# Letting attention run on into the z1 stage, loading spatial weights as their region frees, and two smaller reorderings, in a fused attention and spatial-gating kernel

## The chip, the cores and the metric

One NeuronCore of a Trainium2 chip runs the whole program. The metric is the device time of one execution in microseconds (us), lower is better.

## The reference, cut to what matters

```python
def reference(A_x, A_wqkv, A_wo, B_x, B_w_in, B_w_sp, B_b_sp, B_w_out, gate_w):
    # x: 1 x 2048 x 1024, all bf16
    g = sigmoid((A_x * gate_w).sum(-1, keepdims=True))
    # A: 32 heads of 32, each position attends to 8 positions at distance 0, 2, ... 14
    a = softmax(mask(q . k_gathered * scale)) . v_gathered, then @ wo
    # B: z = gelu(x @ w_in); z1 = first half (1792 columns), z2 = layernorm(second half)
    gsp = w_sp @ z2 + b_sp            # w_sp: 2048 x 2048
    b = (z1 * gsp) @ w_out
    return g * a + (1 - g) * b
```

The kernel runs, in this order: gate and q/k/v products with the scores of attention, z2, z1, the spatial product with w_sp, and the output. TensorE works nearly without a break; attention's weighted sums run beside it on VectorE (DVE), from about 45 to about 300 us.

## The kernel before

All large products are one-level Strassen products: seven smaller products, each of four 128x128 weight loads, whose results are shared and added in PSUM by ScalarE (ACT) and DVE. Every product asks for a bank from `bank_roles`, and ACT copies ("seeds") and evicts between them. A small planner with clocks for each engine interleaves deferred work (`fill`, `due`, `streams`).

**Banks and score blocks.** In group 2 the score blocks stand behind products 1, 3 and 5 of a q/k quad; then the v quads begin:

```python
            if n + 1 in (BAND_AT if g != 2 else (1, 3, 5)):   # BAND_AT = (1, 3, 6)
                band_set(g, x)
# ...
        if g == 2:
            first = v_quad(0)
            for _ in range(2):
                next(first)
                step()
            mark(bank_roles[1][1:3], VH)     # two short matmuls, L558
            run(v_quad(1), first, step=step)
```

**Gate rows.** Two stores of gate rows are issued ahead of everything that follows the first scores:

```python
    sync.dma_start(... g_d ..., g_s[:])
    gate_dma = sync.dma_start(... og_d ..., omg_h[:])
    settle()
    # ... first gathers of scores are planned after this
```

**The z1 stage.** Seven steps (`fp` 0 to 6) of 12.08 us. Attention is forced to end (`drain`) after the second, and the first eight blocks of the spatial weights are loaded with DMA transposes at fixed places of the third, fourth and fifth:

```python
    DRAIN, SUMS = 1, NFH - 2
    RAW_AT = {2: {2: 0, 4: 1}, 3: {2: 2, 4: 3, 6: 4}, 4: {2: 5, 4: 6, 6: 7}}
    for fp in range(NFH):
        # ...
        hooks = {3: lambda: mark(late, 512, ZC),
                 **{n: lambda a=a: load_raw(0, a) for n, a in RAW_AT.get(fp, {}).items()}}
        run(z1_quad(fp, 0), z1_quad(fp, 1), hooks=hooks, step=lambda: z1_step(fp, at))
        if fp == DRAIN:
            drain()
```

Of the kernel before, what the change touches and what calls it, by code (L numbers as in the profile page):

```python
# [13 lines left out]
P = 128  # L14
# [9 lines left out]
NJ = 16  # L24
# [3 lines left out]
ZC = 448  # L28
# [8 lines left out]
NFH = NF // 2  # L37
# [21 lines left out]
def kernel(  # L59
# [34 lines left out]
    g_d = dpool.tile([S], F32, name="g_d")  # L94
# [162 lines left out]
    def dma(ready, dur, f, landed=None, timed=False):  # L257
        if not live[0]:
            return f()
        item = [ready, dur, f, landed, timed]  # L260
        due.append(item)
        return item
# [64 lines left out]
    for i in range(4):  # L327
        vp_tile(i, middle=None)
    band_at = [0]
    last_sub = [None]  # L330
    last_evac = [None]
    BAND_SETS = [(0, 8, 2), (1, 1, 7), (9, 1, 7)]

# [3 lines left out]
    def band_blocks(g, first, step, n, pairs=None):  # L337
# [32 lines left out]
        for q in range(2):  # L370
            for e in range(1 if pairs is None else 2):
                k = n if pairs is None else pairs
                dst = bass.AP(tensor=bd.tensor, offset=bd.offset + (2 * first + 16 * e + q) * BS, ap=[[BR, QB], [2 * step * BS, k], [1, BR]])
                src = st[QB * q:QB * (q + 1), e * k:(e + 1) * k].rearrange("p m k h -> p m (k h)")
                stored[id(st)].append(dma(band_free[0], 0.1 * k, lambda dst=dst, src=src: sync.dma_start(dst, src), landed))

    def band_set(g, x):
        band_blocks(g, *BAND_SETS[x])
# [447 lines left out]
    SQH = 8  # L826
    squares = [(n, x) for n in range(16) for x in range(2)]
    LEAN = (True, True)
    T_START = (0.0, 0.0, 0.0)

    def square(n, x, junk):
        c = slice(x * HF, (x + 1) * HF)
# [50 lines left out]
    def among_bands(g, quad):  # L883
        x = 0
        for n in range(7):
            next(quad)
            step()
            if n + 1 in (BAND_AT if g != 2 else (1, 3, 5)):
                band_set(g, x)
                x += 1  # L890
                step()
        bands_have[0] = g + 1
        next(quad, 0)
# [102 lines left out]
    gate_act = nc.scalar.activation(omg[:], glT, ACT.Tanh, scale=0.5)  # L996
    nc.vector.tensor_scalar(g_s[:], omg[:], 0.5, 0.5, ALU.mult, ALU.add)
    gate_vec = nc.vector.tensor_scalar(omg_h[:], omg[:], -0.5, 0.5, ALU.mult, ALU.add)
    sync.dma_start(bass.AP(tensor=g_d.tensor, offset=g_d.offset, ap=[[P, 16], [1, P]]), g_s[:])
    gate_dma = sync.dma_start(bass.AP(tensor=og_d.tensor, offset=og_d.offset, ap=[[P, 16], [1, P]]), omg_h[:])  # L1000

    settle()
    live[0] = True
    for inst in (gate_mm, gate_act, gate_vec, gate_dma):
        pinned[inst.ins.engine] = inst.ins.name
    for x in clock:
        clock[x] = 0.0
    band_data[0], band_free[0], v_data[0] = T_START
    clock["SP"], clock["DMA"] = 0.5, 1.5
    stored.clear()  # L1010
    bands_have[0] = 1
    next_bands()
    dma(0.0, 0.1, lambda: sync.dma_start(g_att[:], bass.AP(tensor=g_d.tensor, offset=g_d.offset, ap=[[NJ, P], [1, NJ]])))
    next_v(1)
    def load_wvr():
        for m in range(2):
# [8 lines left out]
    for g in range(NG):  # L1025
        main = with_quads(g, group_tiles(g))
        if g in (1, 2, 3, 4):
            load_wqk_later(g + 3, clock["PE"])
        hold[0] = g == NG - 1
        paired = play_group(g)  # L1030
        if not paired:
            play(main[0:8 - (not g)])
        if g == 2:
            first = v_quad(0)
            for _ in range(2):
                next(first)
                step()
            mark(bank_roles[1][1:3], VH)
            run(v_quad(1), first, step=step)
            for i in range(2, 8, 2):  # L1040
                run(v_quad(i), v_quad(i + 1), step=step)
            advance(clock["PE"] + 1.0)
            v_have[0] = NG
            next_v()
            load_later(0, clock["PE"] + 4.0, 6.0)
        if not paired:
            play(main[8 - (not g):])
# [141 lines left out]
    z1_junk = free(BC_OFF, FH)  # L1189
    ready = [0]  # L1190

    def z1_step(fp, at):
        step()
        at[0] += 1
        if at[0] % 2 == 0 and squares:
            act(0.5, clock["PE"])
            square(*squares.pop(0), z1_junk)
        n = ready[0]
        if all(s[1] == () for s in streams) and n + 4 <= (squares[0][0] if squares else 16):
            fill.append((clock["ACT"] + 0.5, 1.0, lambda n=n: moments(n)))  # L1200
            ready[0] += 4
        if fp == NFH - 1 and at[0] == 2:
            fill.extend((0.0, 1.15, f) for f in wsp_sums(0, 1))
# [1 line left out]
    mark([b[1] for b in bank_roles], 512, ZC)  # L1205
    dma(clock["PE"] + 1.0, 2.9, lambda: load_w1(1), w1_landed(1))
    RAW_IN = 3.0
    DRAIN, SUMS = 1, NFH - 2
    RAW_AT = {2: {2: 0, 4: 1}, 3: {2: 2, 4: 3, 6: 4}, 4: {2: 5, 4: 6, 6: 7}}
    for fp in range(NFH):  # L1210
        while w1_left[0]:
            advance(max(clock["PE"], clock["DVE"]) + 0.5)
        if 0 < fp < NFH - 1:
            w1_sums(fp + 1)
        if fp == SUMS:
            fill.extend((clock["PE"] + RAW_IN, 1.15, f) for f in wsp_sums(0, 0))
        late = () if fp else [b[2] for b in bank_roles]
        at = [0]
        hooks = {3: lambda: mark(late, 512, ZC), **{n: lambda a=a: load_raw(0, a) for n, a in RAW_AT.get(fp, {}).items()}}
        if fp == 2:  # L1220
            hooks[6] = lambda: load_w1(5, (0,))
        run(z1_quad(fp, 0), z1_quad(fp, 1), hooks=hooks, step=lambda: z1_step(fp, at))
        if fp == DRAIN:
            drain()
        if fp == 0:
            load_w1(3)
        if fp == 2:
# [379 lines left out]
            load_act(fp // 2 - 1)  # L1607
    out_sums_late()
    traced[0] = len(nc.cur_bb.bb.instructions)
    pinned[gate_dma.ins.engine] = last_store[0].ins.name  # L1610
    for xa in ((1, 1), (0, 1), (0, 0), (1, 0)):
        load_block(1, *xa)
    act_sums(0)
# [46 lines left out]
```

## Time and profile before

| quantity | before |
|---|---|
| median of 3 runs | 650.78 us |
| span of the profiled execution | 648.3 us |
| TensorE busy | 637.5 us |
| the four lines of matmul waits that the prediction adds up | 2.3 us |
| sixth z1 step, first GELU | 331.27, ACT idle 4.68 before it |
| TensorE from the end of the fifth step on | no wait |

The prediction below shows the page's busy lines, the waits and three timelines. A timeline line gives start, duration, engine, line of the kernel, operation, what it writes from what, how many in a row, and in brackets the idle time before it with what ended it. SP's queue (the transposes are the spatial blocks, z_d the z1 stores):

```profile
317.15 1.20 SPq L189 DMA_DIRECT2D z_d<-arena  x2
318.40 9.32 SPq L194 DMA_TRANSPOSE arena<-in_B_w_sp_dram  x3
327.81 1.20 SPq L189 DMA_DIRECT2D z_d<-arena  x2
```

The stores at 327.81 are those of the fifth step; they stand behind three transposes of 3.1 us each. Then ACT and TensorE at the same place, from the same profile:

```profile
326.02 0.57 ACT L486 COPY psum_all<-psum_all 128x512 f32<-128x512 f32 x1 [0.29 <-PE psum_all L402]
331.27 0.60 ACT L1175 ACTIVATE arena<-psum_all 128x512 bf16<-128x512 f32 x1 [4.68 <-DMA z_d<-arena]
...
338.11 0.57 ACT L486 COPY psum_all<-psum_all 128x512 f32<-128x512 f32 x1 [0.29 <-PE psum_all L402]
```

### The profile page before, as it was taken

What the parts mean: (1) busy time and instruction counts of PE and PEld (TensorE: products, weight loads), DVE (VectorE), ACT (ScalarE), POOL (GpSimd) and SP (SyncE); (2) the same over time, 40 slices, a digit from 0 to 9 for tenths busy, and PEclk for the clock granted to TensorE, in tenths of its full rate; (3) what the DMA queues carried; (4) which work ended last, traced back from release to release, by engine and by line L of the source; (5) the groups of instructions that cost most, each with busy time, mean ns of one, the idle gap of its engine ahead of it and who ended that gap; (6) DMA issues with size and microseconds to landing.
All of it is one profiled execution on the core that took longest, in us unless ns stands there. A gap on an engine that the chain in (4) does not pass through costs nothing.

```text
span 648.3 us, 11298 instructions
## 1 busy us (share of the span) xinstructions
PE 637.5 (98%) x4345; PEld 336.2 (52%) x4391; DVE 519.3 (80%) x816; ACT 298.1 (46%) x644; POOL 15.4 (2%) x27
## 2 busy tenths in 40 slices
PE   8999999999999999999999999999999999999997
PEld 4544467444455555444444444444444444868684
DVE  0347998999899999999988766987569999586852
ACT  3547677676786878799643121121121121202120
POOL 2210000000000000001000000000000000000000
PEclk9999999999999999999999999999999999999999
DMA  9979564798687012258994578369487383557501
GB/s 218 202 162 283 115 153 103 175 226 197 133 216 201 1 51 76 66 160 233 259 257 130 130 166 189 100 202 283 91 190 174 84 158 102 107 138 127 124 28 49
DMA packets 227174, 98.19 MB, mean 151 GB/s; under 512 B 174496, under 2 KB 214064, under 8 KB 227120
## 3 DMA queue, kind: packets, MB, share of 16 engines
q1 hardware_dynamic: 226256, 95.70, 61.2%
q0 software_dynamic: 576, 1.57, 0.9%
q8 instruction: 34, 0.56, 0.4%
q10 hardware_dynamic: 288, 0.20, 0.1%
q14 instruction: 20, 0.16, 0.1%
HBM read 44.31 MB, written 36.61 MB: 125 GB/s over the span
## 4 chain that ended last, share of the span: by engine, by line
PE 90%; ACT 4%; SPq 2%; DMA 1%; DVE 1%; issue 1%; DVEq 0%; ACTq 0%
PE psum_all L402 71%; PE psum_all L1484 8%; PE psum_all L293 6%; PE psum_all L303 2%; PE psum_all L355 2%; ACT arena L838 2%; ACT arena L1175 1%; PE psum_all L790 1%; SPq L178 1%; DMA arena<-in_A_wqkv_dram 1%; SPq L194 1%; ACT arena L363 1%; ACT arena L783 1%; DMA arena<-zg_d 1%; DVE psum_all L473 0%
## 5 line engine op out<-in xcount | busy, mean ns | idle before, releaser
L402 PE MATMUL psum_all<-arena 128*128 128x512 f16 (+6 forms) x2481 | 502.5, 362 | 3.3 <-issue 0.8
L402 PEld LDWEIGHTS <-arena 128*128 128x128 f16 (+1 forms) x2518 | 244.9, 98 | 253.4 <-issue 3.2
L676 DVE TENSOR_TENSOR arena<-arena,att_A 128x2048 f16<-128x2048 bf16 x64 | 75.5, 1220 | 0.3
L473 DVE TENSOR_TENSOR psum_all<-psum_all,arena 128x512 f32<-128x512 f32 (+1 forms) x78 | 51.0, 669 | 8.7 <-PE psum_all L402 5.7
L1484 PE MATMUL psum_all<-arena 128*128 128x256 f16 (+1 forms) x468 | 51.6, 273 | 0.0
L1484 PEld LDWEIGHTS <-arena 128*128 128x128 f16 x468 | 45.8, 98 | 5.5
L293 PE MATMUL psum_all<-arena 128*128 128x512 bf16 x183 | 42.0, 379 | 1.2 <-issue 0.8
L420 ACT COPY psum_all<-psum_all 128x512 f32<-128x512 f32 (+1 forms) x24 | 12.5, 519 | 66.2 <-PE psum_all L402 65.5
L783 ACT ACTIVATE arena<-psum_all 128x448 bf16<-128x448 f32 x64 | 34.2, 545 | 18.3 <-PE psum_all L402 9.0
L1175 ACT ACTIVATE arena<-psum_all 128x512 bf16<-128x512 f32 x56 | 31.4, 613 | 19.8 <-PE psum_all L402 9.0
L680 DVE TENSOR_TENSOR arena<-arena 128x2048 f16<-128x2048 f16 x32 | 37.9, 1218 | 0.0
L363 ACT CAST arena<-psum_all 128x1988 f16<-128x1988 f32 (+3 forms) x25 | 33.9, 1358 | 2.7 <-PE psum_all L355 2.3
L838 ACT ACTIVATE arena<-arena 128x896 bf16<-128x896 bf16 x32 | 30.9, 981 | 0.0
L545 DVE TENSOR_TENSOR arena<-arena 128x512 f16<-128x512 bf16 (+5 forms) x60 | 30.1, 534 | 0.4
L444 ACT COPY psum_all<-psum_all 128x512 f32<-128x512 f32 (+1 forms) x24 | 12.3, 518 | 37.5 <-PE psum_all L402 36.8
L293 PEld LDWEIGHTS <-arena 128*128 128x128 bf16 x192 | 18.1, 98 | 21.5 <-DMA arena<-in_A_wqkv_dram 0.6
L869 ACT CAST arena<-psum_all 128x512 bf16<-128x512 f32 x40 | 22.2, 592 | 12.4 <-DVE psum_all L473 9.8
L388 DVE TENSOR_TENSOR arena<-arena 128x2048 f16<-128x2048 bf16 x8 | 9.4, 1221 | 20.9 <-DMA arena<-in_A_x_dram 20.7
L486 ACT COPY psum_all<-psum_all 128x512 f32<-128x512 f32 (+1 forms) x39 | 21.7, 570 | 6.6 <-PE psum_all L402 6.0
L426 ACT COPY arena<-psum_all 128x512 f32<-128x512 f32 (+1 forms) x24 | 12.7, 533 | 26.1 <-PE psum_all L402 22.5
L431 ACT COPY psum_all<-psum_all 128x512 f32<-128x512 f32 (+1 forms) x24 | 12.4, 517 | 25.8 <-PE psum_all L402 24.8
L549 DVE TENSOR_TENSOR arena<-arena 128x1024 f16<-128x1024 f16 (+1 forms) x16 | 11.4, 715 | 15.7 <-PE psum_all L402 15.7
(113 smaller groups left out, 530.3 us busy)
## 6 DMA issues: line engine op xcount, KB each, us to landing
arena<-v_d SPq DMA_DIRECT2D x8, 960.0 KB, 5.8
z_d<-arena SPq DMA_DIRECT2D x14, 512.0 KB, 3.9
arena<-z_d SPq DMA_DIRECT2D x14, 512.0 KB, 4.4
zg_d<-arena SPq DMA_DIRECT2D x56, 128.0 KB, 2.2
arena<-zg_d SPq DMA_DIRECT2D x32, 224.0 KB, 3.2
band_d<-arena SPq DMA_DIRECT2D x28, 248.5 KB, 4.2
arena<-in_A_wqkv_dram SPq DMA_DIRECT2D x16, 256.0 KB, 4.2
o_d<-arena SPq DMA_DIRECT2D x4, 1024.0 KB, 5.7
```

Of the source, the lines that this page charges most:

```text
L293: nc.tensor.matmul(ps[:], w[:, t, kt, :], xT[:, kt, 512 * c:512 * (c + 1)], start=(kt == 0), stop=(kt == KT - 1))
L363: nc.scalar.copy(dst, src)
L402: nc.tensor.matmul(bank[:, 0:N], lhsT, rhs, start=(start and m == 0), stop=(m == n - 1), skip_group_check=True)
L473: last_add[0] = nc.vector.tensor_tensor(out[:, n], a[:, n], vs, ALU.add)
L545: return [lambda a=a: nc.vector.tensor_tensor(*a) for a in args]
L676: lambda ws=ws, in0=in0, in1=in1: tt(p5[:, ws], in0[:, ws], in1[:, ws], ALU.mult)), False
L680: lambda a=p3[:, ws], b=p3[:, ws.start + 4:ws.stop + 4]: tt(a, a, b, ALU.add)), not n
L783: nc.scalar.activation(z2[:, i + 8 * a, ZC * c:ZC * (c + 1)], bank[:, 0:ZC], ACT.Gelu_apprx_tanh, accum_out=s1[:, 4 * n + c:4 * n + c + 1])
L838: return nc.scalar.activation(junk, src, ACT.Square, accum_out=(s2, s2h)[x][:, n:n + 1])
L869: nc.scalar.copy((qT_slots, kT_slots)[t][g % 2][:, :, 256 * (c + 2 * x):256 * (c + 2 * x + 1)], bank[:].rearrange("p (n e) -> p e n", e=2))
L1175: last_gelu[0] = nc.scalar.activation(z1s[:, f, a, :], bank[:], ACT.Gelu_apprx_tanh)
L1484: nc.tensor.matmul(bank[:, h], l, r, start=(start and m == 0), stop=(m == len(ab) - 1), skip_group_check=True)
```

## The change

Its intent: (1) give the first v quad a bank that is free sooner, and put the third score block one product later; (2) issue the first gathers of scores ahead of the gate rows; (3) let attention end in z1 whenever DVE gets to it; (4) since the spatial blocks overwrite a region that attention's last store (o_d) is read from, load them from then on, one every three rounds at the earliest. Part 2 also shifts the planner's start times, which is left out here. Cut to its core:

```diff
-            if n + 1 in (BAND_AT if g != 2 else (1, 3, 5)):
+            if n + 1 in BAND_AT:
 ...
-    sync.dma_start(... g_d ..., g_s[:])
-    gate_dma = sync.dma_start(... og_d ..., omg_h[:])
 ...
     next_bands()
-    dma(0.0, 0.1, lambda: sync.dma_start(g_att[:], ... g_d ...))
+    dma(0.6, 0.1, lambda: sync.dma_start(... g_d ..., g_s[:]))
+    dma(0.6, 0.1, lambda: sync.dma_start(... og_d ..., omg_h[:]))
+    dma(0.6, 0.1, lambda: sync.dma_start(g_att[:], ... g_d ...))
 ...
         if g == 2:
+            r = bank_roles[0]
+            bank_roles[0] = [r[0], r[3], r[2], r[1]]
             first = v_quad(0)
 ...
     def z1_step(fp, at):
         step()
         at[0] += 1
+        since[0] += 1
+        if raws and since[0] >= 3 and not due and all(s[1] == () for s in streams):
+            load_raw(0, raws.pop(0))
+            since[0] = 0
 ...
-    DRAIN, SUMS = 1, NFH - 2
-    RAW_AT = {2: {2: 0, 4: 1}, 3: {2: 2, 4: 3, 6: 4}, 4: {2: 5, 4: 6, 6: 7}}
+    SUMS = NFH - 2
 ...
-        hooks = {3: ..., **{n: lambda a=a: load_raw(0, a) for n, a in RAW_AT.get(fp, {}).items()}}
+        hooks = {3: ...}
 ...
-        if fp == DRAIN:
-            drain()
```

More of the change, by code (lines that the diff above doesn't have):

```diff
@@ L329 @@
     band_at = [0]
-    last_sub = [None]
+    last_band = [None]
     last_evac = [None]
@@ L375, in band_blocks @@
                 stored[id(st)].append(dma(band_free[0], 0.1 * k, lambda dst=dst, src=src: sync.dma_start(dst, src), landed))
+        last_band[0] = stored[id(st)][-1]
     def band_set(g, x):
@@ L828 @@
     LEAN = (True, True)
-    T_START = (0.0, 0.0, 0.0)
+    T_START = (-1.0, 0.0, 3.0)
     def square(n, x, junk):
@@ L998 @@
     gate_vec = nc.vector.tensor_scalar(omg_h[:], omg[:], -0.5, 0.5, ALU.mult, ALU.add)
-    sync.dma_start(bass.AP(tensor=g_d.tensor, offset=g_d.offset, ap=[[P, 16], [1, P]]), g_s[:])
-    gate_dma = sync.dma_start(bass.AP(tensor=og_d.tensor, offset=og_d.offset, ap=[[P, 16], [1, P]]), omg_h[:])
     settle()
     live[0] = True
-    for inst in (gate_mm, gate_act, gate_vec, gate_dma):
+    for inst in (gate_mm, gate_act, gate_vec, last_band[0]):
         pinned[inst.ins.engine] = inst.ins.name
@@ L1008 @@
     band_data[0], band_free[0], v_data[0] = T_START
-    clock["SP"], clock["DMA"] = 0.5, 1.5
+    clock["SP"], clock["DMA"] = -0.5, 0.0
     stored.clear()
@@ L1012 @@
     next_bands()
-    dma(0.0, 0.1, lambda: sync.dma_start(g_att[:], bass.AP(tensor=g_d.tensor, offset=g_d.offset, ap=[[NJ, P], [1, NJ]])))
+    dma(0.6, 0.1, lambda: sync.dma_start(bass.AP(tensor=g_d.tensor, offset=g_d.offset, ap=[[P, 16], [1, P]]), g_s[:]))
+    dma(0.6, 0.1, lambda: sync.dma_start(bass.AP(tensor=og_d.tensor, offset=og_d.offset, ap=[[P, 16], [1, P]]), omg_h[:]))
+    dma(0.6, 0.1, lambda: sync.dma_start(g_att[:], bass.AP(tensor=g_d.tensor, offset=g_d.offset, ap=[[NJ, P], [1, NJ]])))
     next_v(1)
@@ L1190 @@
     ready = [0]
+    raws, since = list(range(8)), [0]
     def z1_step(fp, at):
@@ L1215 @@
         if fp == SUMS:
+            assert not raws
             fill.extend((clock["PE"] + RAW_IN, 1.15, f) for f in wsp_sums(0, 0))
@@ L1218 @@
         at = [0]
-        hooks = {3: lambda: mark(late, 512, ZC), **{n: lambda a=a: load_raw(0, a) for n, a in RAW_AT.get(fp, {}).items()}}
+        hooks = {3: lambda: mark(late, 512, ZC)}
         if fp == 2:
@@ L1609 @@
     traced[0] = len(nc.cur_bb.bb.instructions)
-    pinned[gate_dma.ins.engine] = last_store[0].ins.name
+    pinned[last_store[0].ins.engine] = last_store[0].ins.name
     for xa in ((1, 1), (0, 1), (0, 0), (1, 0)):
```

## The prediction

> **What bounds the kernel now.** I read the page first, then the waits of the TensorE alone, then the timelines around each of them, because the question is how much idle time of the TensorE there is to win.
>
> ```profile
> PE 637.5 (98%) x4345; PEld 336.2 (52%) x4391; DVE 519.3 (80%) x816; ACT 298.1 (46%) x644; POOL 15.4 (2%) x27
> PE   8999999999999999999999999999999999999997
> DVE  0347998999899999999988766987569999586852
> PEclk9999999999999999999999999999999999999999
> ```
>
> The TensorE is busy in every slice but the first and last, at the full granted clock. DVE is nearly full from the third slice to the twentieth (about 30 to 325 us), ACT less so. The waits of the TensorE's matmuls (total us, times, longest) are the whole stock that a reordering can take from, apart from the start:
>
> ```profile
> PE psum_all L402 <- issue: 0.8, 5, 0.2
> PE psum_all L355 <- ACT arena L363: 0.8, 2, 0.6
> PE psum_all L402 <- ACT arena L869: 0.4, 1, 0.4
> PE psum_all L402 <- ACT psum_all L486: 0.3, 1, 0.3
> ```
>
> They sum to 2.3 us of 648.3. Even if all of it went, the time would fall by 0.4%. So this is a question of tenths of a microsecond, and of whether the new order brings a new wait. Three of these places can be touched. The largest lies where group 2's scores end and the v products begin. This is the TensorE there, then ACT (start, duration, engine, line, operation, count, idle before it):
>
> ```profile
> 81.45 0.64 PE L355 MATMUL psum_all<-arena 32*64 32x71 bf16 x56 [0.16 <-ACT arena L363]
> 82.25 2.22 PE L402 MATMUL psum_all<-arena 128*128 128x512 bf16 x11 [0.16 <-issue]
> 84.90 0.70 PE L402 MATMUL psum_all<-arena 128*128 128x320 f16 x4 [0.44 <-ACT arena L869]
> 85.44 0.43 PE L558 MATMUL psum_all<-arena 128*128 128x320 bf16 x2
> ...
> 82.54 1.82 ACT L363 CAST arena<-psum_all 128x1988 f16<-128x1988 f32 x1
> 84.25 1.09 ACT L869 CAST arena<-psum_all 128x512 bf16<-128x512 f32 x2
> 85.20 0.47 ACT L420 COPY psum_all<-psum_all 128x320 f32<-128x320 f32 x1
> ```
>
> The reader should see one chain: the third score block (L355) is evicted by one 1.82 us cast (L363). Behind it in ACT's order stand two evictions of the q/k quad (L869). The v quad's second product wants the bank that the first of these two reads, so it starts 0.44 us late, at 84.90.
>
> The other two places are the end of z2 (0.27 us at 259.09, behind ACT) and the start of the third z1 step (0.27 us at 291.23, behind ACT's L486). There the attention that is forced to end shows on DVE:
>
> ```profile
> 288.42 2.36 DVE L680 TENSOR_TENSOR arena<-arena 128x2048 f16<-128x2048 f16 x2
> 290.81 1.23 DVE L681 TENSOR_TENSOR arena<-arena 128x2048 f16<-128x2048 f16 x1
> 292.07 0.69 DVE L685 TENSOR_TENSOR arena<-arena 128x1024 f16<-128x1024 f16 x1
> 292.68 1.28 DVE L1171 COPY arena<-psum_all 128x512 f32<-128x512 f32 x2
> ...
> 292.79 0.54 SPq L189 DMA_DIRECT2D o_d<-arena  x1
> 298.24 4.37 SPq L194 DMA_TRANSPOSE arena<-in_B_w_sp_dram  x2
> ```
>
> **What the Trainium skill says.** Three places. "Perfetto Trace Analysis", section "Identifying the Most-Contended Engine", says that busy share of matmuls is no measure of distance to the roofline. The trace agrees in that 98% busy stands beside 52% for weight loads, so I count waits, not busy time. "PSUM — Partial Sum Buffer", section "Engine vs sequencer instructions", says that ScalarE's and VectorE's queues are strict FIFO and that matmuls start and end in program order. The trace agrees: L869 sits behind the 1.82 us L363, though its matmuls were over. So what counts is the position in each engine's order. "DMA: Bandwidth & Descriptors", section "Anatomy of one DMA — SWDGE (gpsimd) path", says that a wait on a semaphore is held on the issuing sequencer, not in the DMA engines. The trace agrees for SP too: it issues o_d at 292.79 and then nothing until 298.24, when the first transpose may overwrite the region that o_d is read from.
>
> **The change, part by part.** The built orders have the same instruction counts on PE, DVE, ACT and SP before and after. The TensorE's order differs in one place only: in group 2 the third score block stands behind the quad's sixth product, not its fifth.
>
> *Part 1, roles of the banks and the place of the third score block.* One product of four 512-column matmuls takes 0.863 us (a z1 step of 56 matmuls repeats every 12.08 us in the chain: 300.30, 312.38, 324.47; 12.08/56 = 0.216, times 4). A v product of four 320-column ones takes 0.54 (29.34 us for 216 in the chain). In the new order:
> - Products four to six run from 79.61 to 82.20. The score block starts at 82.29 (0.09 us of changeover, as before). From its start to the next product it needs 0.80 us (81.45 to 82.25 before), so product seven runs 83.09 to 83.95.
> - The first v product ends at 84.50. The second now uses the bank freed by the quad's second eviction, done by about 82.9, so the 0.44 us wait goes; it ends at 85.04.
> - ACT: the exponential (L630, 0.64 us) has moved from an idle slot before the second L363 to just behind it. So ACT runs L363 until 81.40, L630 until 81.94, then three L869 that end at about 82.4, 82.9 and 83.4, and the third L363 from about 83.3 to 85.1 (before: 82.54 to 84.36). Then the last L869 until 85.6 and the v quad's seed copy L420 until about 85.95.
> - The two marking matmuls (L558) write banks that the third L363 reads. They are now due at 85.04 and wait until about 85.17: a new wait of 0.13 us. The second quad's first product ends at 85.98, and the first quad's third product, which needs L420, can start at about 86.0.
> - Before, the same product started at 84.90 + 0.54 + 0.27 + 0.54 = 86.25. The gain is 0.25 us: 0.44 removed, about 0.2 paid back because ACT's work is the same and only better placed.
>
> *Part 2, gate rows behind the score gather.* Before, the gathers are issued at 46.82 and 47.50, behind two stores of gate rows, and the first attention operation on DVE waits for them:
>
> ```profile
> 50.62 0.29 DVE L639 TENSOR_TENSOR att_m<-att_L 128x256 f16<-128x256 f16 x1 [1.93 <-DMA att_L<-band_d]
> ```
>
> Now the gathers can go as soon as the last score store has landed (44.71), and take 2.8 to 3.0 us, so both are there by 48.4. DVE, free at 48.7, gains the 1.9 us. But the exponential still stands behind the quad's L492 on ACT (51.79), and DVE meets its own L473, which waits for the TensorE, at 52.15, 53.96 and 58.75. By 58.75 both orders are level. Nothing on the TensorE waits in this stretch: worth 0.
>
> *Part 3, no forced end in z1.* From 288.5 on DVE now does four weight sums L545 (1.54 us), one L680, then the share copies L1171 at about 291.0 instead of 292.68, then L473, L680, L681 and the second pair of L473 at about 296.0 and 296.6 (before 295.75 and 296.69), then L685 until about 297.9. The attention's end moves by five microseconds, and nothing is removed. The TensorE had no wait at L1171 or L473 here: the accumulation that needs the second L473 comes over 1 us later. The wait at 291.23 is for ACT's seed copy, ACT is full from 273 on with squares and GELUs, and its order is unchanged: that 0.27 us stays. The later DVE order ends level at the last z1 step: its second pair of L473, before at 345.74, comes at about 345.6.
>
> *Part 4, spatial blocks as the region frees.* The o_d store moves from 292.8 to about 298, so the first transpose goes from 298.2 to about 303.5 (o_d holds the region 5.4 us), while the later ones are bunched; at 2.4 to 3 us each with the stores between them the last is out by about 326 (before 327.7). The first DVE operation on them comes at 330.7 before and about 333.5 after. So there is no wait either way: worth 0.
>
> Sum: 650.78 - 0.25 = 650.5. I give the 0.27 us at 291.23 one chance in three to vanish because neighbouring orders shift, which is 0.1 more: 650.4.
>
> **Rivals.** (a) *The z1 reordering delays the TensorE.* For it: DVE is full from 287 to 302 us, and at the last step the read by L473 ends at 346.43 while the matmul that overwrites that bank is due at about 346.5, nearly no margin. Against: my count has DVE level or 0.1 us early there. It would make 651.0 to 651.5. (b) *The second half of z1 weight block 5 comes late*, since it now stands behind the first transpose: it would land at 310 to 312, and its sum is due at 311.9. DVE would wait up to 1 us, but the TensorE has 1.6 us of slack there: 650.4 to 650.8. (c) *The whole stock at ACT's and DVE's chains falls* (0.44 + 0.27 + 0.27, with 0.2 to 0.3 of follow-up at 260 to 263): 649.5. Nothing in the changed order on ACT speaks for it. (d) *Part 1 gains nothing*, the 0.44 us being only moved from the bank to the marking matmuls, as ACT's L630 comes later: 650.8.
>
> **Range and chances.** The three runs before span 650.62 to 651.17, so a median carries about 0.2 us. Rival (c) halfway and (a) halfway bound the rest: 649.7 to 651.1. A change of 2% is 13 us; the waits hold 2.3, and no new chain I can find costs even 1. Faster by over 2%: 0.01; within: 0.98; slower: 0.01.
>
> **What would show it.** Right: no idle before the v quad's second product near 84.5, a short one (0.1 to 0.2) before L558 behind L363; L639 at about 48.7 with the same L473 at 58.75; the wait of about 0.27 at 291 still there, shifted by 0.25; o_d near 298, first transpose near 303.5, no wait of DVE for w_sp. Wrong: TensorE idle near 85.2 of 0.4 or more, TensorE waits for L473 between 292 and 348, or a DVE wait for in_B_w_in at 312.

## More of the kernel before

```profile
321.66 24.55 PE L402 MATMUL psum_all<-arena 128*128 128x512 bf16 x111
```

ACT's first GELU of the sixth step (331.27, ACT idle 4.68 before it) waits for the landing of the fifth step's stores, already in the kernel before. It costs nothing: TensorE runs 24.55 us without a break. The wait is there, but it does not end last.

**Where z1's results wait for their store.** ACT's GELU writes `z1s`, and SyncE (SP) stores it to `z1_d` (named z_d in the profile). There are two pairs of such buffers, but only the fourth step uses the second. So the sixth step's GELUs write where the fifth step's stores read from:

```python
    z1s_slots = [[... for r in range(2)] for o in (T1_OFF, R_OFF + 16384)]
    def z1_quad(fp, c):
        z1s, vs = z1s_slots[fp == 3][c], zv_slots[c]
        # gelu: nc.scalar.activation(z1s[:, f, a, :], bank[:], Gelu)        on ACT
        # store, at the quad's end: sync.dma_start(dst, z1s...)             on SP, in order
```

## The result, and the profile after

| | before | after |
|---|---|---|
| median of 4 runs, same rounds | 650.97 us (650.62 to 652.18) | 652.67 us (652.18 to 653.38) |
| ratio of fast runs | | 1.0024 [1.0006, 1.0041] |
| span of the profiled execution | 648.3 us | 650.4 us |

A ratio is the mean time of one kernel's fast runs over that of the other's of the same rounds, so it is not quite the ratio of the two medians. The class "within 2%" was right. The predicted time, 650.4 us, was not: the kernel became about 1.7 us slower, outside the range of 649.7 to 651.1.

The page of the changed kernel answers to the first lines of the prediction. Nothing is to be seen in the busy shares, and the row of the clock (not shown) is all nines again.

```profile
PE 639.2 (98%) x4346; PEld 336.7 (52%) x4391; DVE 519.6 (80%) x816; ACT 297.4 (46%) x644; POOL 15.8 (2%) x27
```

The waits of TensorE's matmuls (total us, times, longest) show two old lines gone, and three new ones. Lines of code have moved by one here (L403 was L402) and by three in the z1 stage (L1178 was L1175):

```profile
PE psum_all L403 <- ACT arena L1178: 1.0, 3, 0.4
...
PE psum_all L559 <- ACT arena L363: 0.3, 1, 0.3
...
PE psum_all L403 <- ACT psum_all L487: 0.3, 1, 0.3
PE psum_all L403 <- ACT psum_all L421: 0.3, 1, 0.3
```

The longest new one is ACT's GELU (L1178). To find where the time goes, I took the n-th weight load of both traces (4,411 each) and subtracted their starts; I call this the **lag**, positive where the changed kernel is behind:

```
at us (before)   79     85     87     89     181    194    288    306    351    644
lag             +0.02  -0.81  -0.30  +0.13  +0.12  +0.21  +0.21  +0.31  +1.99  +2.07
```

The three waits for L1178 sum to 0.96 us only: the ends of matmuls are modelled in this profile, so a product that is held up bank by bank looks partly busy. Starts are measured, and give more. 1.68 of 2.07 us arise between 306 and 351, in the z1 stage. The kernel wins 0.8 us at 85 and has lost it again by 89.

**Part 1, at 82 to 88 us.** TensorE, then ACT, of the changed kernel:

```profile
82.68 2.12 PE L403 MATMUL psum_all<-arena 128*128 128x512 f16 x12
85.15 0.43 PE L559 MATMUL psum_all<-arena 128*128 128x320 bf16 x2 [0.35 <-ACT arena L363]
85.42 2.34 PE L403 MATMUL psum_all<-arena 128*128 128x320 bf16 x16
88.02 1.25 PE L403 MATMUL psum_all<-arena 128*128 128x320 f16 x8 [0.26 <-ACT psum_all L421]
```

```profile
83.25 1.85 ACT L363 CAST arena<-psum_all 128x1988 f16<-128x1988 f32 x1
84.95 0.63 ACT L870 CAST arena<-psum_all 128x512 bf16<-128x512 f32 x1
85.43 0.48 ACT L421 COPY psum_all<-psum_all 128x320 f32<-128x320 f32 x1
87.22 0.43 ACT L427 COPY arena<-psum_all 128x320 f32<-128x320 f32 x1 [1.30 <-PE psum_all L403]
87.54 0.43 ACT L421 COPY psum_all<-psum_all 128x320 f32<-128x320 f32 x1
```

The 0.44 us before the second v product is gone, and the new wait before the marking matmuls is there (0.35, predicted 0.13). What the prediction did not have is the wait at 88.02. It is for the seed copy L421 at 87.54, which stands on ACT behind the share copy L427, and that one idles 1.30 us. The profile names TensorE as what ended this idle time, but SP's gather of scores starts at 87.26, 0.04 us after L427. In the kernel before the pair is 86.14 and 86.18, and there the profile names the landing of a score store (`band_d`):

```profile
86.14 0.43 ACT L426 COPY arena<-psum_all 128x320 f32<-128x320 f32 x1 [0.46 <-DMA band_d<-arena]
```

The share copy writes to rows that a score buffer also uses, so it may only start when that buffer's store is over; so may the gather. In the changed kernel the pair starts 1.1 us later, while TensorE had come to this place 0.3 us earlier (85.15 against 85.44 at the marking matmuls).

**Part 2** went as predicted: the first attention operation at 48.71, level again at 58.8. The line of before that this answers to is in the prediction.

```profile
48.71 0.29 DVE L640 TENSOR_TENSOR att_m<-att_L 128x256 f16<-128x256 f16 x1
...
52.17 0.70 DVE L474 TENSOR_TENSOR psum_all<-psum_all,arena 128x512 f32<-128x512 f32 x1 [2.22 <-PE psum_all L403]
```

**Part 3** too. DVE's order around 288 us is the predicted one, and the lag stays at +0.21 until 303:

```profile
288.64 1.55 DVE L546 TENSOR_TENSOR arena<-arena 128x512 f16<-128x512 bf16 x4
290.10 1.22 DVE L681 TENSOR_TENSOR arena<-arena 128x2048 f16<-128x2048 f16 x1
291.24 1.28 DVE L1174 COPY arena<-psum_all 128x512 f32<-128x512 f32 x2
```

**Part 4, in the z1 stage.** SP's queue first:

```profile
298.34 0.54 SPq L189 DMA_DIRECT2D o_d<-arena  x1
303.64 2.53 SPq L194 DMA_TRANSPOSE arena<-in_B_w_sp_dram  x1
...
309.14 12.28 SPq L194 DMA_TRANSPOSE arena<-in_B_w_sp_dram  x4
...
326.06 5.14 SPq L194 DMA_TRANSPOSE arena<-in_B_w_sp_dram  x2
331.31 1.20 SPq L189 DMA_DIRECT2D z_d<-arena  x2
```

The o_d store and the first transpose come when the prediction said (298, 303.5). The last transpose leaves at 331.2, not 326, and the fifth step's stores stand behind it at 331.31, 3.5 us later than before. They also take longer to land: the first GELU starts 4.94 us after this issue, and did so 3.46 us after it in the kernel before. ACT and TensorE pay for it:

```profile
336.25 0.60 ACT L1178 ACTIVATE arena<-psum_all 128x512 bf16<-128x512 f32 x1 [9.35 <-DMA z_d<-arena]
337.49 3.53 ACT L1178 ACTIVATE arena<-psum_all 128x512 bf16<-128x512 f32 x7 [0.64 <-DMA z_d<-arena]
340.85 1.15 ACT L487 COPY psum_all<-psum_all 128x512 f32<-128x512 f32 x2
```

```profile
336.90 1.02 PE L403 MATMUL psum_all<-arena 128*128 128x512 bf16 x3 [0.30 <-ACT arena L1178]
338.14 1.02 PE L403 MATMUL psum_all<-arena 128*128 128x512 bf16 x4 [0.22 <-ACT arena L1178]
339.61 6.65 PE L403 MATMUL psum_all<-arena 128*128 128x512 f16 x29 [0.44 <-ACT arena L1178]
```

ACT's idle time of 4.68 us has become 9.35 us. Eight GELUs that were spread between products now run in one row until 340.85, and TensorE's seventh step needs the banks that they read. DVE meets the same lateness on the other side, at the first sum of the spatial weights:

```profile
335.35 1.23 DVE L1136 TENSOR_TENSOR arena<-arena 128x2048 f16<-128x2048 bf16 x1 [1.47 <-DMA arena<-in_B_w_sp_dram]
```

That wait of DVE costs nothing here, because ACT is later still.

**Theory S**: the whole z1 loss comes from SP's row of transposes ending later, by way of the stores that queue behind them. **Rivals**: W, the loads' own lateness (DVE's wait for w_sp) is enough to hold TensorE by itself; R, the attention that now runs into z1 costs DVE time by itself.

### The profile page after: what moved, and what is told of

It reads as the page before. It is cut to its first block, busy times and chain, and to the rows that moved or that the text cites. A ratio compares the mean times of both kernels' runs of the same rounds, so it can differ in the third digit from the quotient of the medians.

```text
span 650.4 us, 11298 instructions
## 1 busy us (share of the span) xinstructions
PE 639.2 (98%) x4346; PEld 336.7 (52%) x4391; DVE 519.6 (80%) x816; ACT 297.4 (46%) x644; POOL 15.8 (2%) x27
## 4 chain that ended last, share of the span: by engine, by line
PE 88%; ACT 5%; SPq 2%; DVE 2%; DMA 1%; issue 1%; ACTq 0%; DVEq 0%
PE psum_all L403 68%; PE psum_all L1491 8%; PE psum_all L293 6%; PE psum_all L303 2%; ACT arena L1178 2%; PE psum_all L355 2%; ACT arena L839 1%; SPq L194 1%; DMA z_d<-arena 1%; PE psum_all L791 1%; SPq L178 1%; DMA arena<-in_A_wqkv_dram 1%; ACT arena L363 1%; ACT arena L784 1%; DVE psum_all L474 1%
## 5 line engine op out<-in xcount | busy, mean ns | idle before, releaser
L403 PE MATMUL psum_all<-arena 128*128 128x512 f16 (+6 forms) x2482 | 503.5, 362 | 4.1 <-ACT arena L1178 1.0
L403 PEld LDWEIGHTS <-arena 128*128 128x128 f16 (+1 forms) x2518 | 245.1, 98 | 254.9 <-issue 5.6
L474 DVE TENSOR_TENSOR psum_all<-psum_all,arena 128x512 f32<-128x512 f32 (+1 forms) x78 | 51.1, 670 | 11.5 <-PE psum_all L403 8.3
L293 PE MATMUL psum_all<-arena 128*128 128x512 bf16 x183 | 42.0, 379 | 1.2 <-issue 0.8
L421 ACT COPY psum_all<-psum_all 128x512 f32<-128x512 f32 (+1 forms) x24 | 12.5, 521 | 65.9 <-PE psum_all L403 65.3
L1178 ACT ACTIVATE arena<-psum_all 128x512 bf16<-128x512 f32 x56 | 31.2, 615 | 22.5 <-DMA z_d<-arena 10.0
L363 ACT CAST arena<-psum_all 128x1988 f16<-128x1988 f32 (+3 forms) x25 | 34.0, 1360 | 3.3 <-PE psum_all L355 2.8
L293 PEld LDWEIGHTS <-arena 128*128 128x128 bf16 x192 | 18.1, 98 | 21.4 <-DMA arena<-in_A_wqkv_dram 0.6
L870 ACT CAST arena<-psum_all 128x512 bf16<-128x512 f32 x40 | 22.1, 592 | 12.5 <-DVE psum_all L474 9.6
L427 ACT COPY arena<-psum_all 128x512 f32<-128x512 f32 (+1 forms) x24 | 12.7, 534 | 27.4 <-PE psum_all L403 23.8
L303 PE MATMUL psum_all<-arena 128*128 128x385 bf16 x128 | 22.8, 334 | 0.3 <-DVE arena L325 0.3
```

Of the source, the lines that this page charges most:

```text
L293: nc.tensor.matmul(ps[:], w[:, t, kt, :], xT[:, kt, 512 * c:512 * (c + 1)], start=(kt == 0), stop=(kt == KT - 1))
L303: nc.tensor.matmul(ps[:, 0:VP + 1], xT[:, kt, i * P:(i + 1) * P], wvp[:, kt, :], start=(kt == 0), stop=(kt == KT - 1))
L363: nc.scalar.copy(dst, src)
L403: nc.tensor.matmul(bank[:, 0:N], lhsT, rhs, start=(start and m == 0), stop=(m == n - 1), skip_group_check=True)
L474: last_add[0] = nc.vector.tensor_tensor(out[:, n], a[:, n], vs, ALU.add)
L1178: last_gelu[0] = nc.scalar.activation(z1s[:, f, a, :], bank[:], ACT.Gelu_apprx_tanh)
```

## The experiments

Eleven runs were made, on three chips (b, c, d), each beside runs of the kernel before on the same chip. All results were correct. The table gives for every trace what the lag to the first trace of before gains in three stretches, beside DVE's wait for one gather of scores near 170 us (in us):

| run | chip | median (before) | ratio [95%] | 79 to 89 | DVE's wait near 170 | 181 to 194 | 306 to 351 |
|---|---|---|---|---|---|---|---|
| before, first trace | a | 650.97 | | 0 | 2.17 | 0 | 0 |
| after, first trace | a | 652.67 (650.97) | 1.0024 [1.0006, 1.0041] | +0.11 | 2.26 | +0.09 | +1.68 |
| e1 z1 parts alone | b | 655.10 (651.44) | 1.0053 [1.0028, 1.0077] | 0.00 | 2.77 | +1.04 | +1.90 |
| e2 all but z1 parts | b | 652.07 (651.44) | 1.0008 [0.9991, 1.0024] | +0.15 | 2.86 | +0.77 | 0.00 |
| e3 own rows | b | 654.41 (651.44) | 1.0041 [1.0022, 1.0060] | +0.40 | 2.85 | +1.12 | +1.97 |
| e4 bank roles alone | b | 652.52 (651.44) | 1.0009 [0.9991, 1.0028] | -0.52 | 3.04 | +1.05 | 0.00 |
| f1 before, again | c | 653.44 (652.18) | 1.0009 [0.9986, 1.0032] | 0.00 | 2.79 | +0.74 | 0.00 |
| f2 after, again | c | 656.31 (652.18) | 1.0054 [1.0028, 1.0079] | +0.28 | 3.63 | +2.35 | +3.88 |
| f3 fixed loads | c | 653.59 (652.18) | 1.0021 [1.0000, 1.0041] | +0.12 | 3.52 | +1.49 | +0.80 |
| f4 gate rows alone | c | 654.90 (652.18) | 1.0036 [1.0010, 1.0061] | +0.23 | 4.05 | +2.54 | 0.00 |
| g1 own rows and fixed loads | d | 651.83 (651.54) | 1.0010 [0.9985, 1.0035] | +0.09 | 3.02 | +1.01 | 0.00 |
| g2 bank roles alone, again | d | 651.91 (651.54) | 1.0008 [0.9983, 1.0034] | -0.54 | 3.06 | +1.00 | 0.00 |
| g3 forced end, free loads | d | 656.84 (651.54) | 1.0083 [1.0061, 1.0104] | +0.02 | 2.52 | +0.34 | +3.37 |

Single runs of one kernel differ by 2 to 5 us on chips b to d, more than most of what is looked for; so the lag by stretch decides, and the ratio is the check.

**e1: the z1 parts alone**, put into the kernel before (parts 3 and 4, nothing else).

```diff
-    RAW_AT = {2: {2: 0, 4: 1}, 3: {2: 2, 4: 3, 6: 4}, 4: {2: 5, 4: 6, 6: 7}}
-        if fp == DRAIN:
-            drain()
+        if raws and since[0] >= 3 and not due and all(s[1] == () for s in streams):
+            load_raw(0, raws.pop(0))
```

> The kernel before with the z1 part of the change alone (no forced end of attention, spatial blocks as the region frees); banks, third score block, gate rows and start clocks as before. Theory S (store slot): the whole loss is made here, as the stores of the fifth z1 step stand behind three late transposes on SP and the GELUs of the sixth step wait for their landing: 1.4 to 1.8 us slower than before, with TensorE waits for the GELU line at the start of the seventh step. Rival G (groups 0 to 2): most of the loss is made by the bank roles and the gate rows: then this run is within 0.3 us of before.

The z1 stage loses 1.90 us, ACT idles 9.56 us for z_d, and TensorE waits for L1175 three times, 1.2 us in all. Of its six runs, three at clock 1.000 took 652.76 to 654.37, and three at 0.997 took 655.84 to 657.92. Parts 3 and 4 by themselves are enough.

**e2: the changed kernel with the z1 parts undone** (the edit of e1 in reverse, made in the changed kernel).

> The changed kernel with its z1 part undone; gate rows, start clocks, bank roles and score block as in the change. Theory S: within 0.3 us of before (the traces show a lag of 0.13 us at 88 us and 0.21 at 192). Rival G: 1 us or more slower than before.

The z1 stage loses nothing. Together with e1 this puts the whole stretch down to parts 3 and 4. It is no faster than the kernel before: parts 1 and 2 gain nothing that can be seen.

**e3: the sixth step's GELUs into rows of their own**, so that they need not wait for the fifth step's stores. The rows are free until two other loads need them, which go one step later.

```diff
+    z1x = [free(BC_OFF + 2048 * c, 2048)... for c in range(2)]
-        z1s, vs = z1s_slots[fp == 3][c], zv_slots[c]
+        z1s, vs = (z1x if fp == 5 else z1s_slots[fp == 3])[c], zv_slots[c]
-        if fp == NFH - 3:
+        if fp == NFH - 2:
             load_rows()
```

> The changed kernel, where the sixth z1 step puts its GELU results into a place of its own (the rows of the two vectors, which are loaded one step later for it), so it no longer waits for the stores of the fifth step. The transposes stay as late as in the change. Theory S: the TensorE waits for the GELU line at the seventh step vanish, 1.4 to 1.7 us faster than the changed kernel, so about 0.2 us slower than before. Rival W (late w_sp blocks): DVE's 1.5 us wait for the spatial blocks at 335 us delays its copies of the seventh step, and most of the loss stays: over 652.

What theory S expected did not happen. ACT's wait is gone (its first GELU starts at 331.84), but the stretch loses 1.97 us all the same. DVE, then TensorE:

```profile
337.48 1.23 DVE L1136 TENSOR_TENSOR arena<-arena 128x2048 f16<-128x2048 bf16 x1 [2.35 <-DMA arena<-in_B_w_sp_dram]
```

```profile
345.35 3.61 PE L403 MATMUL psum_all<-arena 128*128 128x512 f16 x16 [0.60 <-DVE psum_all L474]
350.02 2.32 PE L403 MATMUL psum_all<-arena 128*128 128x512 f16 x10 [1.06 <-DVE psum_all L474]
```

So W is right as well. The wait of DVE for the last spatial block, which looked harmless in the changed kernel, stood hidden behind ACT's, and holds TensorE by itself. It need not be as expensive there: in this trace the last transpose leaves 0.9 us later, counted from TensorE (333.3 at a lag of 1.56, against 331.2 at 0.31), and DVE waits 2.35 us for it and not 1.47. Theory S, in the form that the store alone holds TensorE, fell; the new form is S+W: one cause (the row of transposes ends too late) and two consequences, of which the later one shows.

**f1 and f2: both kernels again, unchanged**, as controls on another chip.

> The kernel before, unchanged, as a control on the chip of the other three: its time against itself shows what a difference of medians is worth on this chip, and its trace how late the score gather lands and whether the TensorE waits for DVE near 53 and 190 us here too. Expected: ratio 1.000 within 0.002.

> The changed kernel, unchanged, on the same chip. Expected as on the first chip: 1.5 to 2 us slower than before, with TensorE waits for the GELU line of about 1 us in sum at the start of the seventh z1 step.

The unchanged kernel before lags its own first trace by 3.46 us: 2.7 at the start, mostly in waits for the load of x, and 0.74 near 190 us. So much can differ between two executions of one kernel. The z1 stage is not part of it: 0.00. The changed kernel loses 3.88 us in z1, more than twice as much as in its first trace, and in this trace one sees why. TensorE, then the granted clock (PEclk) by stretches of 2 us:

```profile
340.82 1.02 PE L403 MATMUL psum_all<-arena 128*128 128x512 bf16 x4 [1.41 <-ACT arena L1178]
342.34 4.83 PE L403 MATMUL psum_all<-arena 128*128 128x512 bf16 x14 [0.50 <-ACT arena L1178]
```

```profile
core 0: us, PE busy (x) PEld busy (x) DVE busy (x) ACT busy (x) POOL busy (x), PEclk, DMA share, GB/s
...
342.00:344.00 2.00, 1.66 (x4) 0.55 (x4) 1.97 (x3) 2.00 (x5) 0.00 (x0) 0.57 0.76 203
344.00:346.00 2.00, 2.00 (x7) 0.76 (x6) 0.86 (x2) 2.00 (x5) 0.00 (x0) 0.57 0.19 76
```

After two waits, 1.41 and 0.50 us, eight matmuls follow each other at 0.43 us (the first at 0.38) and not 0.216, at a clock of 0.57 in each of the two stretches. The lag grows from 5.36 to 6.99 in them, 1.63 us. The Trainium skill ("TensorE: Matmul & The Clock Gate", section "What's actually happening") says that the array runs at half clock after an idle window of about 3.4 us, and that the window runs free of the kernel. The half clock agrees. The length of idle time does not: here 1.9 us in two pieces were enough, and in g3 below a wait of 3.21 us was followed by full clock. So the wait has a price of its own and a second one by lot. An episode of 1.63 us in a span of 655.3 is 0.0025 of it, the size of the drop from 1.000 to 0.997; I read the other runs at 0.997 in the same way, but only this one has a trace that shows it. They are not evenly spread: of the 33 runs of the kernel before that stood beside the experiments two have 0.997, of e1's six three, of f4's six three, and of g3's seven all but the profiled one 0.995 to 0.997.

**f3: no forced end, but loads at fixed places again**, three blocks in the fourth step and five in the fifth.

```diff
-        if raws and since[0] >= 3 and not due and all(s[1] == () for s in streams):
-            load_raw(0, raws.pop(0))
-            since[0] = 0
-        hooks = {3: ...}
+        RAW_AT = {3: {2: 0, 4: 1, 6: 2}, 4: {1: 3, 2: 4, 4: 5, 5: 6, 6: 7}}
+        hooks = {3: ..., **{n: lambda a=a: load_raw(0, a) for n, a in RAW_AT.get(fp, {}).items()}}
```

> The changed kernel with the forced end still gone, but the spatial blocks at fixed places again: three in the fourth z1 step, five in the fifth, none ahead of the stores of the third step and none ahead of the second weight half of block 5. Theory P (place of the blocks): the late o_d store alone costs nothing, because eight blocks of about 2.9 us from 303.6 us with the stores between end near 328.5, the stores of the fifth step go at about 328.6 and the GELUs of the sixth step start near 333, early enough: no TensorE wait for the GELU line, 1.5 us faster than the changed kernel. Rival E (the end of attention): any order that lets attention end late delays the chain, and at least 1 us of the loss stays.

The loss in z1 falls to 0.80, DVE waits no more for w_sp, and TensorE's wait for L1178 is one of 0.41 us. It is not gone, because the last transpose still leaves at 332.1 on a TensorE that is 1.8 us behind the first trace. In this trace the place of the loads takes away about half of the loss. Neither expectation was met: theory P had no wait left, rival E at least 1 us.

**g1: own rows and fixed loads together** (the edits of e3 and of f3).

> The changed kernel with both repairs together: the spatial blocks loaded at fixed places (three in the fourth step, five in the fifth) and the sixth step's GELUs written to rows of their own. Theory S+W (two waits stacked one behind the other: ACT's GELU for the fifth step's stores, and behind it DVE for the last spatial block; both come from the stretched row of transposes, nothing else in the new z1 order costs anything): both waits are gone, ACT shows no wait for z_d at the sixth step's first GELU, DVE none for in_B_w_sp, and the lag of the TensorE against the kernel before changes by less than 0.2 us between 303 and 350 us (it was +1.7 in the changed kernel, +0.76 with fixed loads alone, +1.97 with own rows alone); time against the changed kernel of other runs 1.5 to 2.5 lower, so a ratio to the kernel before of about 1.001. Rival R (the later attention on DVE costs by itself, whatever the loads do): the TensorE still waits 0.5 to 1.5 us there, for DVE's L473/L474 line.

This is the run that decides. The timeline of TensorE from the end of the third step to past the end of the seventh has one line:

```profile
299.68 52.70 PE L403 MATMUL psum_all<-arena 128*128 128x512 f16 x243
```

The lag changes by 0.00 between 306 and 351. Alone, one repair left 1.97 and the other 0.80; both together leave nothing. R is refuted: attention still runs on into z1 here, and costs nothing there (0.08 to 0.09 us of lag arise between 303 and 306 us in this trace and in the other five without a forced end, and none in those with one).

The trace does not show that both repairs are needed. The same fixed loads were faster in this execution than in f3: the last transpose left at 329.7 at a lag of 0.98, which is 1.6 us earlier counted from TensorE. What it shows besides is how long ACT waits at this place when no store holds it:

```profile
331.26 0.60 ACT L1179 ACTIVATE arena<-psum_all 128x512 bf16<-128x512 f32 x1 [3.69 <-PE psum_all L403]
```

So of ACT's 4.68 us in the kernel before, 3.69 are for TensorE's product, and only 1.0 for the stores. How much later the GELUs could have been follows from three traces. Counted from TensorE (lag at 306 us taken off), the first GELU of the sixth step came 4.67 us later than before in the changed kernel, 4.88 in e1 and 3.81 in f3, and TensorE lost 1.68, 1.90 and 0.80: the margin was 3.0 us each time. By this estimate the fixed loads alone would have been in time in g1's execution: its stores left SP 1.0 us later than before, counted from TensorE, and even with 1.5 us more to land that is below 3.0.

The five of g1's six runs at clock 1.000 have a median of 651.56 us, the seven such runs of the kernel before on that chip 651.54.

**g3: the forced end put back, loads left free.**

```diff
         run(z1_quad(fp, 0), z1_quad(fp, 1), hooks=hooks, step=lambda: z1_step(fp, at))
+        if fp == 1:
+            drain()
```

> The changed kernel with the forced end put back and the loads left free (as the region frees). Theory S (the harm comes from the o_d store being late, so the row of transposes starts and ends late): o_d is back near 293, the first transpose near 298, the last is out by 327 or earlier, no wait of ACT for z_d over 5 us, no TensorE wait at the seventh step for L1178. But now the transposes follow each other so early that the second half of z1 weight block 5 stands behind one and lands near 316: DVE then waits 3 to 4 us for it near 312, and the TensorE loses 1 to 3 us at the fifth or sixth step. Rival F (the free loads alone do the harm at the seventh step): the wait for L1178 is still there, 1 us or more.

```profile
317.70 1.55 DVE L546 TENSOR_TENSOR arena<-arena 128x512 f16<-128x512 bf16 x4 [5.50 <-DMA arena<-in_B_w_in_dram]
```

```profile
322.42 5.77 PE L403 MATMUL psum_all<-arena 128*128 128x512 f16 x26 [3.21 <-DVE psum_all L474]
```

As expected, and larger: the free loads now fill SP's queue from 298.41, the second half of z1's weight block 5 stands behind five transposes, DVE waits 5.50 us for it and TensorE 3.21. The seventh step has no wait for L1178, but this says less than hoped, since TensorE arrives there 3.4 us later anyhow. Six of the seven runs have a clock of 0.995 to 0.997 and took 656.64 to 658.26; the profiled one, at 1.000, took 653.37. This shows that the order in which SP's queue is filled costs z1 time in either arrangement; only what is made to wait differs.

**e4 and g2: the bank roles alone**, in the kernel before.

```diff
         if g == 2:
+            r = bank_roles[0]
+            bank_roles[0] = [r[0], r[3], r[2], r[1]]
             first = v_quad(0)
```

> The kernel before with the exchanged bank roles for the v quads alone; the third score block stays behind the fifth product. Theory: the wait of 0.44 us at the v quad's second product goes and no other comes, as the exponential stays in ACT's idle slot and the third eviction of scores ends at 84.4 us, before the marking matmuls are due: 0.4 us faster than before, about 650.5. Rival: ACT is the bound there, and the wait only moves to the marking matmuls or to the third product: within 0.1 us of before.

> The kernel before with the exchange of the bank roles alone, again on another chip: in its first run the local wait of 0.44 us at the v quad's second product was gone with no new one (lag -0.52), and a wait for DVE near 190 us took it back. If that wait comes only from the run's spread in the landing of a score gather near 170 us, a trace with that DVE wait below 2.3 us keeps the gain: 0.4 to 0.5 us faster than the kernel before, ratio 0.9993. If the exchange itself makes the later gather land late, the DVE wait near 170 is again 3.0 or more and the gain is gone: ratio 1.0005 or more.

In both traces the exchange wins 0.52 and 0.54 us by 89 us and keeps it until 181. In the whole time this cannot be seen: near 190 us both runs lose 1.0 us again. Of g2's two alternatives the second came true (DVE's wait 3.06 us, ratio 1.0008), which it had put down to the exchange making the later gather land late. Two traces with the exchange alone (3.04, 3.06) against three without any change before 190 us (2.17 to 2.79) do not settle that.

The seven traces that have all of part 1 show +0.02 to +0.40 at 89, so something takes the gain back. It goes by way of the seed copy behind the share copy, which idles for a landing (1.21 to 1.59 us in the five of them where the trace names it). The moved score block looks like the cause, but all seven also have part 2, and no run has the moved block without it. The run with part 2 alone (f4, next) has the block in its old place, and shows the late share copy too:

```profile
87.23 0.43 ACT L427 COPY arena<-psum_all 128x320 f32<-128x320 f32 x1 [1.21 <-DMA band_d<-arena]
```

With each trace's lag at 79 us taken off, the share copy starts at 86.1 to 86.8 in the five traces without part 2 and at 87.1 to 87.5 in the eight with it. So part 2 is at least as likely to take the gain back; the run that would decide, the exchange and part 2 with the block in its old place, was not made. Why the landing comes later is not settled either.

**f4: the gate rows alone** (part 2 in the kernel before, with the planner's start times that go with it).

```diff
-    sync.dma_start(... g_d ..., g_s[:])
-    gate_dma = sync.dma_start(... og_d ..., omg_h[:])
     next_bands()
+    dma(0.6, 0.1, lambda: sync.dma_start(... g_d ..., g_s[:]))
+    dma(0.6, 0.1, lambda: sync.dma_start(... og_d ..., omg_h[:]))
```

> The kernel before with part 2 alone: gate rows behind the first score gather and the new start clocks. My view now: where the gather lands in time (first chip) it is worth 0; where it lands late, DVE's attention is up to 1.9 us ahead, the TensorE's waits for DVE near 53 and 190 us shrink, and it is 0.3 to 1 us faster than before on the same chip. Rival: the start of attention never matters, ratio 1.000.

The expectation failed. The kernel came out slower. It loses 0.23 us at 79 to 89: ACT's exponential (L631) stands behind the second L363 here, as in all traces with part 2 and in none without, and the wait for L870 is 0.68 us where it was 0.44. Most is lost near 190 us:

```profile
191.99 4.25 PE L403 MATMUL psum_all<-arena 128*128 128x448 f16 x20 [2.09 <-DVE psum_all L474]
```

Between 165 and 192 us DVE has one break only, its wait for one gather of scores near 170. All these kernels have it, and its length differs from run to run. Read the two columns of the table together: a wait of 2.2 us costs nothing, and about what it is longer by, sometimes more, TensorE loses near 190 (3.04 gives 1.05, 4.05 gives 2.54). The kernel before has it too (2.79 and 0.74 in f1). The eight traces that contain part 2 have 2.26 to 4.05, the five without 2.17 to 3.06: they overlap, and though the three longest are all with part 2, these are also three of the four runs of chip c. Whether part 2 makes that landing later stays open.

## Why the prediction was wrong

**Bound and method.** That TensorE is the bound and that waits count, not busy shares, held: 2.07 us of lag are in a handful of short waits, while the busy share stayed at 98%. The stock of 2.3 us was read wrongly, though. Its line "issue" (0.8 us, five times), like a second such line of 0.8 us for L293 that was left out, is very likely not idle time but missing records. The eleven later traces have 4,391 matmuls recorded and not 4,345, and no "issue" wait; and f1, the same kernel, passes two of these places (79.61, 82.25) in the same time as the first trace, with a lag of 2.73 us at 79 and at 85.

**Part 1 (predicted -0.25).** The removed 0.44 holds, and so does the new wait behind L363: 0.35 us in place of 0.13, ending at 85.15 (predicted 85.17). It is longer because TensorE was there at 84.80 and not at 85.04: from the start of the score block to the next product it takes 0.58 us (82.10 to 82.68), and the 0.80 of the prediction very likely contained a missing record (f1 has 0.57 there, 84.19 to 84.76). The exponential's new place on ACT, which the prediction counts under part 1, comes from part 2 (f4). The step "the first quad's third product, which needs L420, can start at about 86.0" was reckoned for the first quad only. The second quad's third product needs the same kind of copy, and ACT had a landing in front of it. Result of parts 1 and 2 together +0.11; the exchange of banks alone gave -0.52 and -0.54. Rival (d), that part 1 gains nothing, was right in its result, by another wait than it named.

**Part 2 (predicted 0)** came as told at 48 to 59 us, and its price at 79 to 89 (0.23 us in f4) was not foreseen. **Part 3 (predicted 0)** came as told, to 0.1 us.

**Part 4 (predicted 0) is the step that failed**: "at 2.4 to 3 us each with the stores between them the last is out by about 326 [...] So there is no wait either way". Two things in it were wrong. First the size: the eight transposes held SP for 2.53 + 12.28 + 3.29 + 5.14 = 23.24 us, 2.9 each, and the loads and stores between them for another 3.8, so the row that began at 303.64 ended at 331.2. I had given it 22.5 us in all. The sum does not follow from its own terms: eight blocks at 2.4 to 3 us and 3.8 between them end at 326.5 to 331.3, and in the trace of before the eight had taken 24.79 us. Second the consequence: I asked only who reads the transposed blocks (DVE, where "no wait" was forecast and 1.47 us came) and not who stands behind them in the same queue. The fifth step's stores stood there, and ACT, which idled 4.68 us before the first GELU behind them already in the kernel before, idled 9.35. That line was in the trace of before. I had passed it over since it cost nothing. Of it TensorE lost 1.68 us in this trace, 1.90 in e1, and with a stretch of half clock 3.88 in f2.

**Rivals.** (a) named the place (z1 reordering); its size was too small (651.0 to 651.5; the kernel took 652.67), and it gave DVE and L473 as the carrier; in the changed kernel it is ACT and L1178. Only e3 makes DVE's L474 the carrier, once ACT's wait is gone. (b) did not occur in the changed kernel and did in g3. (c) did not occur.

**Range.** A wait of several microseconds off the critical path was treated as worth nothing, without asking how much longer it could grow. The margin there was 3.0 us. The stores left SP 3.5 us later and took 1.5 us more to land, and that was enough.

No version was found that beats both kernels by more than chance: g1 and g2 are level with the kernel before.

## What to carry to other kernels

When a change delays or bunches transfers, list everything that stands behind them in the same issuing queue, and who waits for those, not only who reads what they bring. A wait that costs nothing in the profile of before may grow only so far before TensorE feels it. Its own length does not say how far (here ACT idled 4.68 us, and the margin was 3.0): look for when the waiting engine's result is first needed, write the difference down and compare each delay with it. And when one wait is removed and the time does not move, look for a second one that had been hidden behind the first, and remove both before judging the theory.

## What the Trainium skill lacked or had wrong

- "TensorE: Matmul & The Clock Gate", section "What's actually happening", gives an idle window of about 3.4 us before the clock is halved. Here two waits of 1.41 and 0.50 us were followed by eight matmuls at 0.43 us each (clock 0.57 over 4 us, 1.63 us lost), and in another run a wait of 3.21 us was followed by full clock. How much idle time, in several pieces, is enough is not given.
- "DMA: Bandwidth & Descriptors", section "Latency and other measured facts", gives 261 GB/s for a DMA transpose with a non-contiguous middle dimension. Here eight blocks of 128x2048 bf16 (4.19 MB) took 23.24 us of SP's queue, which is 180 GB/s, with other transfers beside them.
- I found no page that says how long a DMA transpose of this size from HBM holds the trn2 queue that issues it: 2.9 us on SP here, where plain loads and stores beside it took 0.5 to 1.2 us each, so what stands behind it comes late by that much.
- No page that I found says how far the landing of one and the same transfer varies from run to run: DVE's wait for one gather was 2.17 and 2.79 us in two traces of the unchanged kernel, and 0.74 us of TensorE came of it.
